# Logits of all heads in one TensorE step, PSUM handed out bank by bank, zero matmuls at the start

## The chip, the cores and the metric

The kernel runs on one core of one Trainium2 chip. The metric is device time in microseconds of one execution. A core has five engines that run side by side: TensorE (PE in the profile, with PEld for its weight loads), VectorE (DVE), ScalarE (ACT), GpSimd (POOL) and SyncE (SP, which here only issues DMAs). Matmuls write to PSUM, 128 partitions by eight banks; a bank holds 512 float32 per partition. VectorE and ScalarE copy results from PSUM to SBUF, the core's working memory.

## The reference

Two layers, each an attention block A and a gated mixing block B, both with a residual connection. The weights are the same in both layers.

```python
def _A_ref(x, wqkv, wo):              # x: 1 x 2048 x 576
    H = 32; Dh = 18; W, dil = (8, 2)
    qkv = (x @ wqkv).reshape(B, S, 3, H, Dh).transpose(2, 0, 3, 1, 4)
    q, k, v = qkv[0], qkv[1], qkv[2]
    idx = pos[:, None] - (arange(W) * dil)[None, :]     # 8 keys: t, t-2, ..., t-14
    mask = idx >= 0
    ...
    logits = einsum('bhsd,bhswd->bhsw', q, kg) * Dh ** -0.5
    attn = softmax(where(mask, logits, -1e9))
    o = einsum('bhsw,bhswd->bhsd', attn, vg)
    return o.transpose(0, 2, 1, 3).reshape(B, S, D) @ wo

def _B_ref(x, w_in, w_sp, b_sp, w_out):   # Fh = 2304
    z = gelu(x @ w_in)
    z1, z2 = z[..., :Fh], layernorm(z[..., Fh:])
    g = einsum('ts,bsf->btf', w_sp, z2) + b_sp[None, :, None]
    return (z1 * g) @ w_out

for _ in range(2):
    x = x + _A_ref(layernorm(x), A_wqkv, A_wo)
    x = x + _B_ref(layernorm(x), B_w_in, B_w_sp, B_b_sp, B_w_out)
```

All arrays are bfloat16; accumulation is float32.

## The kernel before

The program has five parts in a row: `phase_F(0)`, `phase_S(1)`, `phase_F(2)`, `phase_S(3)`, `phase_E()`.

**Phase F** holds, for one layer: the layer norm of x (16 row tiles of 128), the projections to q, k and v, the windowed attention, the output projection with the residual, a second layer norm, and z2 = gelu(x @ w_in) for the second half of w_in with its own layer norm. In layer two it begins with the last projection of block B of layer one (`p3_steps`). **Phase S** computes z1 and g = w_sp @ z2 for nine column blocks and multiplies them. **Phase E** is the last projection to the output.

Attention goes over 18 query tiles of 114 rows (each tile with a halo of 14 rows before it), in nine groups of two. Since the dilation is 2, even and odd rows (`par`) are independent and have 57 queries and 64 keys each. Head dimension 18 is laid on four row groups of 32 partitions, eight heads to a group. To bring q and k into that layout, `QK_steps` writes the projections to a DRAM buffer (`qk_bounce`) and reads them back as `QK`.

What sets the order is `Flow`, a planner that runs on the host while the program is built. Each piece of work is a `step` with an engine, a cost in microseconds, a key (its priority), the steps it comes after, and the buffers it takes and uses. `order()` places one step after another on the engine that is free first; `Plan` holds the keys' offsets, one set for each phase F. Phase S is written out by hand.

The steps that the change and the prediction touch:

- **Logits** (`Lm`, lines 615 to 628). For each query tile there are 64 matmuls of 18 x 64 keys against 18 x 57 queries, one for each of eight heads `g`, four row groups `j` and two parities; each goes to row group 32 j and to the upper or lower 64 columns of the array. They come in two steps, `La` for row groups 0 and 1 and `L` for 2 and 3, each with a PSUM buffer of two banks. Then follow exp on ScalarE (`x0`, `x1`), the mask on VectorE (`k`), P·V on TensorE (`v`, line 647) and the division by the sum (`f`).
- **PSUM** comes from a pool with two tags: `H`, three buffers of two banks, and `PT`, two buffers of one bank (`Ht`, `PTt`, `bank`, lines 256 to 263). The pool hands the buffers of a tag out in rotation. The planner counts how many are taken (`room`, `placed`), not which.
- **Waits**: the framework makes one instruction wait for another where they touch the same tile. `wrote_xn` and `read_xn_strided` (lines 242 to 254) drop waits between columns of `xnD` that do not overlap.
- **q and k, last 64 columns** (`mm4`, line 538): one bank's worth, in an `H` buffer.
- **g in phase S** (line 900): two halves of 16 matmuls each into the two banks of one `H` buffer; then for each half VectorE adds the bias (line 905) and multiplies by z1 (line 906).
- **p3** (line 362): 2 x 18 matmuls into an `H` buffer, 288 columns in each bank, then VectorE adds the residual (line 407). The last tile of phase E is added and stored in two halves.
- **Layer norm** (`ln_steps`): statistics on VectorE, small operations on GpSimd, normalisation on ScalarE, five transposes on TensorE (line 325), a copy by VectorE or ScalarE (lines 342 and 343, the lines of all such copies).

At the start VectorE's queue holds three small memsets, three memsets of the v buffers (line 801), and then the first statistics.

Of the kernel before, what the change touches and what calls it, by code (L numbers as in the profile page):

```python
# [18 lines left out]
P = 128  # L19
# [28 lines left out]
PLANS = (Plan(LX=4, LW=3.41, LR=3.7, KQ=4.95, KX=12.29,  # L48
              KV=2.02, KL=2.15, KE=22.44, KM=1.86, KP=2.02, KF=13.34, KY=2.53, KZ=15.66, KS=0.73, STAY=0.73, LF=4.38),
         Plan(LX=5.14, LW=3.5, LR=4.76, KQ=4.29, KX=10.53,  # L50
              KV=0.36, KL=2.04, KE=1.11, KM=0, KP=0.18, KF=6.22, KY=4.16, KZ=15.99, KS=0.47, STAY=0.73, LF=3.89))
# [3 lines left out]
class Flow:  # L55
# [31 lines left out]
    def room(self, st):  # L87

        t, more = 0.0, {}
        for tag, _ in st["takes"]:  # L90
            more[tag] = more.get(tag, 0) + 1
        for tag, n in more.items():
            ends = self.ends.setdefault(tag, [])
            left = self.caps[tag] - self.held.get(tag, 0) - n
            if left < 0:
                return None
            if left < len(ends):
                t = max(t, ends[-1 - left] + self.LAG)
        return t

    def placed(self, st):

        for tag, b in st["takes"]:
            self.held[tag] = self.held.get(tag, 0) + 1
            self.tag[b] = tag
        for b in st["uses"]:
            self.rest[b] -= 1
            self.last[b] = max(self.last.get(b, 0.0), st["end"])
            if not self.rest[b]:
                self.held[self.tag[b]] -= 1  # L110
                insort(self.ends.setdefault(self.tag[b], []), self.last[b])
# [8 lines left out]
    def order(self):  # L120
        free, mode = {}, {}
        self.ends, self.held, self.tag, self.last = {}, {}, {}, {}
# [64 lines left out]
    def issue(self):  # L187
        for st in self.order():
            st["fn"](st.get("arg", st["on"]))


class K:
# [17 lines left out]
    def setup(self):  # L210
# [4 lines left out]
        self.ps = ctx.enter_context(tc.tile_pool(name="ps", bufs=1, space=PSUM))  # L215
# [7 lines left out]
        make_identity(nc, self.ident[:])  # L223
        nc.vector.memset(self.neg_half[:], -0.5)
# [17 lines left out]
    def wrote_xn(self, ins, c0, c1):  # L242
# [4 lines left out]
        self.xn_writes.append((ins.ins, c0, c1))  # L247

    def read_xn_strided(self, ins, c0, c1):

        self.tc.declare_no_dep(ins.ins, group="xn_writes", keep=[w for w, a, b in self.xn_writes if a < c1 and c0 < b],
# [4 lines left out]
    def Ht(self, name):  # L256
        return self.ps.tile([P, 2, 512], f32, name=name, tag="H", bufs=3)

    def PTt(self, name):
        return self.bank(name)[:].bitcast(bf16)[:, 0:5 * P].rearrange("p (c n) -> p c n", n=P)  # L260

    def bank(self, name):
        return self.ps.tile([P, 512], f32, name=name, tag="PT", bufs=2)
# [29 lines left out]
    def ln_steps(self, fl, tag, key, row0, x, after, uses=(), guard=()):  # L293
# [27 lines left out]
        def trans(_):  # L321
            tp, xn = self.PTt("ln_tp"), box["xn"]
            box["tp"] = tp
# [5 lines left out]
        def evac(e):  # L329
            self.wrote_xn(self.copy(e, self.xnD[:, 0:5, cols], box["tp"][:, :, :n]), cols.start, cols.stop)  # L330
# [14 lines left out]
    def p3_steps(self, fl, i, key, wout, x_prev, x, takes, last):  # L345
# [8 lines left out]
        def mms(hh, part):  # L354
            def f(_):
                if hh == 0 and part == 0:
                    box["ps"] = self.Ht("p3_ps")
# [54 lines left out]
    def phase_F(self, li):  # L412
# [9 lines left out]
        fl = Flow(dict(H=3, PT=2, QK=3, bn=2, stg=6, xt=NX, xn=3, ln_st=6, o_t=2), pl.STAY, self.pairs, pl.LF)  # L422
# [84 lines left out]
        def QK_steps(g, key):  # L507
# [9 lines left out]
            for d in range(NM):  # L517
                def mm(rest_first, d=d):
                    ps = box[d] = self.Ht("qk_ps")
# [18 lines left out]
            def mm4(_):  # L538
                ps = box[NM] = self.Ht("qk4_ps")
                for c in range(NM + 1):  # L540
                    lhsT = wqk[:, c, NM * P:NM * P + P] if c < NM else wqk_r[:, NM * P:NM * P + P]
                    nc.tensor.matmul(ps[:, 0, 0:gw], lhsT=lhsT, rhs=self.xnD[:, c, at], start=(c == 0), stop=(c == NM))

            def ev4(e):
                box[NM, "s"] = stage()[:, 0:gw].rearrange("p (r j) -> p r j", r=2)
                self.copy(e, box[NM, "s"], box[NM][:, 0, 0:gw].rearrange("p (j r) -> p r j", r=2))
# [4 lines left out]
            fl.step(f"{tag}.m{NM}", "PE", 0.05 + 0.0021 * gw, key, mm4, feeds(c0, gw) + ["wqk", "wzero"],  # L551
                    takes=[("H", f"{tag}.ps{NM}")], mode="w", pairs=5)
# [22 lines left out]
        def V_steps(t, key):  # L575
            box, v = {}, vb[t % 3]

            def mm(rest_first):
                ps = box["ps"] = self.Ht("v_ps")
                c0 = QT * t  # L580

                def part(first, wide):
                    for c in range(NM) if wide else (NM,):
                        for s in range(2):
                            for par in range(2):
# [7 lines left out]
                                    tile_position=(rows.start, to.start)), c0, c0 + P)  # L593
# [15 lines left out]
        def ATT_steps(t, key):  # L609
# [5 lines left out]
            def Lm(a):  # L615
                def f(_):
                    qk = self.QKs[group[t]]
                    ps = box["L", a] = self.Ht("L_ps")
                    for g in (0, 2, 1, 3, 4, 6, 5, 7):
                        for par in range(2):  # L620
                            for j in (2 * a, 2 * a + 1):
                                rows = slice(32 * j, 32 * j + DH)
                                at, to = HP * (g // 2 % 2), 4 * par + 2 * (g // 4) + g % 2
                                nc.tensor.matmul(ps[at:at + HP, j % 2, to * QH:(to + 1) * QH],  # L624
                                                 lhsT=qk[rows, g, 1, par, kb:kb + HP],
                                                 rhs=qk[rows, g, 0, par, kb + HALO // 2:kb + HALO // 2 + QH],
                                                 start=True, stop=True, tile_position=(32 * j, at))
                return f
# [12 lines left out]
            def pv(_):  # L641
                O = box["O"] = self.Ht("O_ps")
# [8 lines left out]
            def fin(_):  # L651
# [10 lines left out]
            fl.step(tag + ".x0", "ACT", 0.92, key - pl.KE, ex(0), [tag + ".La", "fills"] + ([f"a{t - 2}.v"] if t > 1 else []), [tag + ".L0"],  # L662
                    mode="x")
            fl.step(tag + ".x1", "ACT", 0.92, key - pl.KE, ex(1), [tag + ".x0", tag + ".L"], [tag + ".L1"], mode="x")
# [6 lines left out]
            def tr(_):  # L671
                tp, o_t = self.PTt("o_tp"), box["o"]
# [19 lines left out]
        def W_steps(i):  # L692
# [5 lines left out]
            def wm(hh):  # L698
                def f(_):
                    if hh == 0:  # L700
                        box["ps"] = self.Ht("w_ps")
# [21 lines left out]
        def Z2_steps(i, key, after):  # L723
# [5 lines left out]
            def mm(u):  # L729
                def f(rest_first):  # L730
                    ps = box[u] = self.Ht("z_ps")
# [72 lines left out]
        fl.step("masks", "POOL", 2.0, -16, lambda _: fills(1), ["fills"] + (["lnx8.p"] if first else []))  # L804
        for i in range(NS):
# [16 lines left out]
        for i in range(NS):  # L822
            Z2_steps(i, pl.KZ + pl.KS * i, [f"win2.{k}" for k in range(len(win2_parts()))] +
                     ([] if first else [f"p3_{j}.m11" for j in range(NS)]))
        with tc.manual_schedule():
            fl.issue()
        self.pairs = fl.pairs
# [11 lines left out]
    def phase_S(self, li):  # L839
# [21 lines left out]
        for jj in range(NB):  # L861
# [7 lines left out]
            H3 = [self.Ht("z1_ps") for _ in range(3)]  # L869
            out = [[t[:, h, :] for h in range(2)] for t in H3]  # L870
            out.append([self.bank("z1_bank")[:] for _ in range(2)])
# [24 lines left out]
            for q in (range(4) if jj < NB - 1 else (3, 2, 1, 0)):  # L896
                ps = self.Ht("g_ps")
# [13 lines left out]
    def phase_E(self):  # L911
# [5 lines left out]
        fl = Flow(dict(H=3, x=4, ob=3))  # L917
# [9 lines left out]
        for i in range(NS):  # L927
            self.p3_steps(fl, i, i, wout, self.xres[1], lambda i=i: x_tile(i), [("x", f"x{i}")], True)
        with tc.manual_schedule():
            fl.issue()  # L930
        cm.__exit__(None, None, None)
# [57 lines left out]
```

## Time and profile before

| what | value |
|---|---|
| three runs | 1224.11, 1230.03, 1230.40 us, median 1230.03 |
| the profiled execution's own time | 1226.56 us |
| its span, first to last instruction | 1224.8 us |
| mean granted clock of TensorE | 0.997 |
| DMA traffic | 75.09 MB, mean 61 GB/s |

The profile shows one execution. In a row of the timeline stand: start and length in us, engine, line, operation, tile written and read, shape, count, and in brackets the idle time before it with what ended it. A matmul's row is longer than its share of TensorE: the matmuls overlap, so the cost of a group is read from its start to the next group's start. In a row of waits stand: who waited for whom, the total in us, how often, and the longest. "Granted clock" is the share of its full clock that TensorE was allowed. A wait for several things is put down to the one that came last.

### The profile page before, as it was taken

Reading aid. Unit: us, or ns where it says so; the run is one execution under the profiler, and the core shown is the slowest. Engines: PE = TensorE matmul, PEld = TensorE weight load, DVE = VectorE, ACT = ScalarE, POOL = GpSimd, SP = SyncE. Lnnn points to the kernel's source line nnn. Section 1 sums busy time; section 2 is a strip of 40 time slices with the busy share of each in tenths; the row PEclk is TensorE's granted clock in tenths of the full one; section 3 lists DMA queues with packets and bytes.
Section 4 is the critical chain, followed back from the end, with each engine's and each line's share of the span. In section 5 each row is a group of like instructions: output and inputs, shape, how many; then the busy total and the mean of one; then the engine's idle time right before and its main releaser. Section 6 shows DMA issues by size and latency. Waiting matters only on the chain.

```text
span 1224.8 us, 25328 instructions
## 1 busy us (share of the span) xinstructions
PE 1196.8 (98%) x10942; PEld 679.3 (55%) x10942; DVE 551.4 (45%) x894; ACT 396.8 (32%) x683; POOL 200.4 (16%) x492
## 2 busy tenths in 40 slices
PE   6899999999999999999999999999999999999998
PEld 4677655444444444448777776554444444444576
DVE  7787865423322232333466877652322332232311
ACT  6765687510011111003454767772111101111000
POOL 6211267400000000012111125671000000000000
PEclk9999999999999999999999999999999999999999
DMA  7655209430000000033323361088000000001121
GB/s 199 133 132 142 56 21 207 87 86 1 10 11 10 10 10 1 1 106 92 74 61 68 91 164 44 16 171 199 11 10 10 1 10 10 10 1 36 33 69 50
DMA packets 139649, 75.09 MB, mean 61 GB/s; under 512 B 96544, under 2 KB 136672, under 8 KB 139536
## 3 DMA queue, kind: packets, MB, share of 16 engines
q1 hardware_dynamic: 138864, 71.01, 24.5%
q0 software_dynamic: 672, 2.45, 0.8%
q8 instruction: 86, 1.41, 0.5%
q14 instruction: 27, 0.22, 0.1%
HBM read 39.54 MB, written 17.11 MB: 46 GB/s over the span
## 4 chain that ended last, share of the span: by engine, by line
PE 91%; DVE 3%; DMA 2%; ACT 1%; POOL 1%; SPq 1%; issue 1%; POOLq 0%; DVEq 0%
PE g_ps L900 41%; PE p_ps L362 11%; PE z_ps L288 11%; PE z_ps L876 8%; PE qk_ps L288 4%; PE w_ps L703 3%; PE v_ps L588 3%; PE z_bank L876 3%; PE z_ps L282 2%; PE O_ps L647 2%; DVE v_ext L342 1%; PE z_ps L882 1%; ACT v_ext L343 1%; PE ln_tp L325 1%; DMA QK<-qk_bounce 1%; PE qk_ps L282 1%
## 5 line engine op out<-in xcount | busy, mean ns | idle before, releaser
L900 PE MATMUL g_ps<-W,zu 128*128 128x512 bf16 x2304 | 500.2, 379 | 0.0
L900 PEld LDWEIGHTS <-zu 128*128 128x128 bf16 x2304 | 225.2, 98 | 272.1
L905 DVE TENSOR_TENSOR g_tmp<-g_ps,bsp 128x512 f32<-128x512 f32 x144 | 99.1, 688 | 432.4 <-PE g_ps L900 432.4
L892 ACT ACTIVATE zu<-z_ps 128x1024 bf16<-128x1024 f32 x54 | 51.4, 1025 | 516.0 <-PE z_ps L882 508.5
L362 PEld LDWEIGHTS <-zu 128*128 128x128 bf16 x1152 | 112.1, 98 | 32.1 <-DVE zu L906 2.1
L288 PE MATMUL z_ps<-wA,xnD 128*128 128x384 bf16 x576 | 109.8, 327 | 0.0
L362 PE MATMUL p_ps<-wA,zu 128*128 128x288 bf16 x768 | 105.8, 286 | 1.3 <-DVE v_ext L342 0.6
L906 DVE TENSOR_TENSOR zu<-g_tmp,zu 128x512 bf16<-128x512 f32 x144 | 99.7, 692 | 11.2 <-DVE g_tmp L905 0.5
L288 PEld LDWEIGHTS <-xnD 128*128 128x128 bf16 x768 | 70.9, 98 | 56.5 <-issue 14.6
L876 PE MATMUL z_ps<-xnD,w 128*128 128x512 bf16 x432 | 96.2, 378 | 0.0
L876 PEld LDWEIGHTS <-w 128*128 128x128 bf16 x576 | 54.2, 97 | 71.8 <-issue 8.0
L740 ACT ACTIVATE zu<-z_ps 128x768 bf16<-128x768 f32 x96 | 77.2, 805 | 33.0 <-PE z_ps L282 18.0
L750 DVE CUSTOM_DVE_ANT_1 zu<-zu 128x1536 bf16<-128x1536 bf16 x32 | 56.6, 1768 | 49.5 <-ACT zu L740 49.5
L288 PE MATMUL qk_ps<-xnD,wqk 128*128 128x242 bf16 x576 | 73.4, 274 | 3.5 <-ACT xnD L343 1.0
L632 ACT ACTIVATE P<-L_ps 128x912 bf16<-128x912 f32 x72 | 64.5, 940 | 7.1 <-PE L_ps L624 6.9
L308 POOL TENSOR_SCALAR ln_st<-ln_st 128x1 f32<-128x1 f32 x64 | 19.5, 304 | 273.9 <-DVE ln_st L304 226.3
L288 PEld LDWEIGHTS <-wqk 128*128 128x128 bf16 x576 | 54.2, 100 | 15.6 <-issue 9.9
L319 ACT ACTIVATE xn<-zu,ln_st 128x512 bf16<-128x512 bf16 (+1 forms) x56 | 33.3, 646 | 64.9 <-POOL ln_st L310 63.9
L801 POOL MEMSET v_ext<- 128x1216 bf16 x3 | 3.2, 1107 | 301.5 <-PE g_ps L900 301.5
L319 ACT ACTIVATE xn<-xt,ln_st 128x512 bf16<-128x512 bf16 x72 | 42.5, 646 | 23.8 <-POOL ln_st L310 23.8
L703 PE MATMUL w_ps<-wo,oT 128*128 128x288 bf16 x320 | 45.9, 293 | 2.0 <-DVE v_ext L342 1.5
L288 PE MATMUL z_ps<-wB,xnD 128*128 128x384 bf16 x192 | 46.9, 326 | 0.0
(88 smaller groups left out, 1141.1 us busy)
## 6 DMA issues: line engine op xcount, KB each, us to landing
qk_bounce<-stg SPq DMA_DIRECT2D x72, 121.0 KB
QK<-qk_bounce SPq DMA_DIRECT2D x72, 121.0 KB
w<-in_B_w_in_dram SPq DMA_DIRECT2D x36, 128.0 KB
wA<-in_B_w_in_dram SPq DMA_DIRECT2D x12, 288.0 KB
wA<-in_B_w_out_dram SPq DMA_DIRECT2D x4, 864.0 KB
xres<-xt SPq DMA_DIRECT2D x18, 144.0 KB
x<-xres SPq DMA_DIRECT2D x16, 144.0 KB
out_dram<-ob SPq DMA_DIRECT2D x15, 144.0 KB
```

The source lines that it names most:

```text
L288: nc.tensor.matmul(ps(s), lhsT=lhsT, rhs=rhs, start=(c == 0 and not rest_first), stop=(c == NM - 1 and rest_first))
L319: nc.scalar.activation(out=out, in_=in_, func=ACT.Identity, scale=rstd[:n], bias=nmr[:n])
L362: nc.tensor.matmul(ps[:, hh, 0:288], lhsT=u[:, s * S + i * P:s * S + (i + 1) * P], rhs=wout(b, s)[:, hh * 288:(hh + 1) * 288], start=(b == ...
L632: nc.scalar.activation(out=Psb[:, 2 * hh:2 * hh + 2, :, 0:QH], in_=box["L", hh][:, :, 0:8 * QH].rearrange("p a (b c) -> p a b c", c=QH), f ...
L703: nc.tensor.matmul(box["ps"][:, hh, 0:288], lhsT=oT[:, c, at:at + P], rhs=wo[:, c, hh * 288:(hh + 1) * 288], start=(c == 0), stop=(c == 4))
L740: nc.scalar.activation(out=self.zu[:, 3 * u:3 * u + 3, 256 * i:256 * (i + 1)].rearrange("p j (s r) -> p s j r", s=2), in_=box[u][:, :, 0:3 ...
L750: nc.vector.tensor_tensor_reduce(out=junk(0, 6), in0=z[:, 0:6, :], in1=z[:, 0:6, :], scale=1.0 / FH, scalar=0.0, op0=ALU.mult, op1=ALU.add ...
L876: nc.tensor.matmul(out[q][h], lhsT=w1[:, NM * h + c, :], rhs=self.xnD[:, c, PADL + 512 * q:PADL + 512 * q + 512], start=(first and c == 0) ...
L892: nc.scalar.activation(out=uq, in_=H3[q][:], func=ACT.Gelu_apprx_tanh)
L900: nc.tensor.matmul(ps[:, s, :], lhsT=z2[:, i, s, :], rhs=W[q][:, i, :], start=(i == 0), stop=(i == NS - 1))
L905: nc.vector.tensor_tensor(out=tmp[:], in0=ps[:, s, :], in1=bsp[:, 512 * q:512 * (q + 1)], op=ALU.add)
L906: nc.vector.tensor_tensor(out=uv, in0=tmp[:], in1=uv, op=ALU.mult)
```

## The change

1. `Lm(0)` and `Lm(1)` become one step `L` with both PSUM buffers. The loops are turned round so that eight matmuls in a row go to eight different places of the array: four row groups and two column halves.
2. PSUM is one tile of eight banks. The planner keeps the end time of each bank, picks the bank (`PT`) or the aligned pair (`H`) for each step in its computed order, and the step asks for what it was given. Any of the four pairs can be an `H` buffer and any bank a `PT` buffer. `mm4` takes one bank. Where waits on `xnD` are dropped, the writers whose PSUM bank a v projection takes over are kept. In phase S, which has no planner, the same rotation as before remains: pairs 0, 2, 4 and banks 6, 7.
3. Nineteen matmuls of zeros (12, 3 and 4) are put before the first layer norm's transposes, between the first and the second, and after the second. A memset of their operand comes first on VectorE.
4. The two plans' offsets are new.

```diff
+PLANS = (Plan(LX=4, LW=3.41, LR=3.7, KQ=5.26, KX=10.68,
+              KV=2.36, KL=2.02, KE=19.35, KM=1.6, KP=1.68, KF=13.78, KY=3.31, KZ=15.55, KS=0.38, STAY=0.5, LF=4.38),
...
+    def open_banks(self, tag):
+        w, f = 2 if tag == "H" else 1, self.bank_end
+        return [(max(f[k:k + w]), k) for k in range(0, 8, w) if None not in f[k:k + w]]
...
+            if tag in ("H", "PT"):
+                f = self.bank_end
+                fit = [(e, k) for e, k in self.open_banks(tag) if e + self.LAG <= st["start"] + 1e-9]
+                if tag == "H":
+                    k = min(fit)[1]
...
-        self.ps = ctx.enter_context(tc.tile_pool(name="ps", bufs=1, space=PSUM))
+        self.psum = ctx.enter_context(tc.tile_pool(name="ps", bufs=1, space=PSUM)).tile([P, 8, 512], f32, name="psum")
+        self.flow, self.turn = None, [0, 0]
...
+        self.idle = self.zu[:, NB, 0:512]
+        nc.vector.memset(self.idle, 0.0)
...
+    def banks(self, kind):
+        if self.flow is not None:
+            return self.flow.given(kind)
+        k = self.turn[kind == "PT"]
+        self.turn[kind == "PT"] += 1
+        return 6 + k % 2 if kind == "PT" else 2 * (k % 3)
+
+    def Ht(self):
+        b = self.banks("H")
+        self.last_bank = b
+        return self.psum[:, b:b + 2, :]
...
-                    for g in (0, 2, 1, 3, 4, 6, 5, 7):
-                        for par in range(2):
-                            for j in (2 * a, 2 * a + 1):
-                                rows = slice(32 * j, 32 * j + DH)
-                                at, to = HP * (g // 2 % 2), 4 * par + 2 * (g // 4) + g % 2
+                for g in (0, 1, 4, 5):
+                    for par in range(2):
+                        for s in range(2):
+                            for j in range(4):
+                                rows, gs = slice(32 * j, 32 * j + DH), g + 2 * s
+                                at, to = HP * s, 4 * par + 2 * (g // 4) + g % 2
...
-            fl.step(tag + ".La", "PE", 0.34, key - pl.KL, Lm(0), [f"qk{group[t]}a"] + ([f"a{t - 1}.L"] if t else []),
-                    [f"QK{group[t]}"], takes=[("H", tag + ".L0")], mode="q", pairs=H)
-            fl.step(tag + ".L", "PE", 0.34, key - pl.KL, Lm(1), [tag + ".La", f"qk{group[t]}"], [f"QK{group[t]}"], takes=[("H", tag + ".L1")],
-                    mode="q", pairs=H)
+            fl.step(tag + ".L", "PE", 0.36, key - pl.KL, Lm, [f"qk{group[t]}a", f"qk{group[t]}"], [f"QK{group[t]}"],
+                    takes=[("H", tag + ".L0"), ("H", tag + ".L1")], mode="q", pairs=2 * H)
...
+                    for k in range(n):
+                        nc.tensor.matmul(ps[:, k % 2, :], lhsT=self.idle[:, 0:P], rhs=self.idle, start=True, stop=True)
+                return f
+            for k, (n, cost, pre) in enumerate(((12, 5.2, []), (3, 0.7, ["lnx0.t", "spin0"]), (4, 0.9, ["lnx1.t", "spin1"]))):
+                fl.step(f"spin{k}", "PE", cost, -100, turn(n), pre, ["spin"] if k else [],
+                        takes=[] if k else [("H", "spin")], mode="w", pairs=n)
```

More of the change, by code (lines that the diff above doesn't have):

```diff
@@ L188, in issue, with given @@
         for st in self.order():
+            self.give = [(tag, self.bank_of[b]) for tag, b in st["takes"] if tag in ("H", "PT")]
             st["fn"](st.get("arg", st["on"]))
+    def given(self, kind):
+        tag, k = self.give.pop(0)
+        assert tag == kind
+        return k
 class K:
@@ L254, in read_xn_strided, with PTt, bank @@
         self.xn_strided.append((ins.ins, c0, c1))
[L256 to L263, printed above, removed]
+    def banks(self, kind):
[8 more added lines that the diff above has]
+        return self.psum[:, b:b + 2, :]
+    def PTt(self):
+        return self.bank().bitcast(bf16)[:, 0:5 * P].rearrange("p (c n) -> p c n", n=P)
+    def bank(self):
+        b = self.last_bank = self.banks("PT")
+        return self.psum[:, b, :]
     def load576(self, main, rest, lo, up, engs):
@@ L641, in pv @@
             def pv(_):
[L642 removed]
+                O = box["O"] = self.Ht()
                 for h in range(8):
@@ L671, in tr @@
             def tr(_):
-                tp, o_t = self.PTt("o_tp"), box["o"]
+                tp, o_t = self.PTt(), box["o"]
                 box["tp"] = tp
```

106 lines of the change are left out of this document (66 added, 40 removed).

## The prediction

> **What bounds the kernel now.** I read the page's first part and its chain of waits, then one table of stretches, then single stages.
>
> ```profile
> span 1224.8 us, 25328 instructions
> PE 1196.8 (98%) x10942; PEld 679.3 (55%) x10942; DVE 551.4 (45%) x894; ACT 396.8 (32%) x683; POOL 200.4 (16%) x492
> PE 91%; DVE 3%; DMA 2%; ACT 1%; POOL 1%; SPq 1%; issue 1%; POOLq 0%; DVEq 0%
> ```
>
> TensorE is busy 98% of the span and makes 91% of the chain. Time can come from three places only: less TensorE work, TensorE work at a better clock, or the 28 us in which it stands. The stretches below follow the phases: start, two pieces of fill, attention, the z2 matmuls, the mixing phase S, then the same for layer two, and the last projection. Columns: length, then busy time (and instructions) of PE, PEld, DVE, ACT, POOL, granted clock, DMA share, GB/s.
>
> ```profile
> core 0: us, PE busy (x) PEld busy (x) DVE busy (x) ACT busy (x) POOL busy (x), PEclk, DMA share, GB/s
> 0.00:8.00 8.00, 0.00 (x0) 0.00 (x1) 5.13 (x12) 2.15 (x3) 2.68 (x12) 1.00 0.79 211
> 8.00:28.00 20.00, 18.34 (x178) 13.38 (x178) 15.81 (x43) 15.18 (x28) 14.63 (x46) 1.00 0.79 203
> 28.00:46.00 18.00, 15.12 (x363) 11.13 (x361) 13.71 (x26) 13.10 (x22) 8.22 (x20) 0.91 0.63 123
> 46.00:148.00 102.00, 96.98 (x2288) 75.30 (x2287) 82.61 (x144) 64.70 (x102) 13.96 (x36) 0.98 0.52 119
> 148.00:228.00 80.00, 80.00 (x562) 42.42 (x561) 47.78 (x64) 63.92 (x142) 55.26 (x133) 1.00 0.42 89
> 228.00:548.50 320.50, 320.50 (x1513) 142.53 (x1512) 96.66 (x144) 36.35 (x49) 9.48 (x22) 1.00 0.12 29
> 548.50:603.00 54.50, 53.74 (x476) 42.84 (x475) 24.62 (x50) 17.70 (x28) 9.48 (x27) 1.00 0.35 97
> 603.00:748.00 145.00, 140.03 (x2925) 110.42 (x2923) 105.14 (x184) 85.52 (x130) 25.86 (x57) 1.00 0.40 92
> ...
> 1149.00:1224.78 75.78, 71.07 (x577) 56.17 (x575) 14.96 (x21) 0.00 (x0) 0.00 (x0) 0.99 0.18 56
> ```
>
> The z2 stretch and phase S have no idle TensorE, so nothing the change does to waits can help there. The idle time sits in the first 46 us (8.0 + 1.7 + 2.9), in the two attention stretches (5.0 each), at the start of layer two (0.8) and in the last stretch (4.7).
>
> **Part 1, the logits.** Before, a step issues 32 matmuls for two head columns; after, one step issues 64 over all four row groups and both column halves.
>
> ```profile
> 46.41 0.69 PE L647 MATMUL O_ps<-v_ext,P 128*64 128x38 bf16 x32
> 46.94 1.15 PE L588 MATMUL v_ps<-wv,xnD 128*64 128x288 bf16 x16
> ...
> 48.27 0.73 PE L624 MATMUL L_ps<-QK 18*64 18x57 bf16 x64
> 48.94 0.45 PE L675 MATMUL o_tp<-ident,o_t 128*128 128x128 bf16 x5
> ...
> 99.82 0.45 PE L624 MATMUL L_ps<-QK 18*64 18x57 bf16 x31
> 100.20 0.45 PE L675 MATMUL o_tp<-ident,o_t 128*128 128x128 bf16 x5
> ```
>
> From start to the next start, 64 logits matmuls cost 48.94 - 48.27 = 0.67 us and 32 cost 0.38, so 32 more cost 0.29: 9.1 ns each, with 0.09 fixed. The P·V matmuls above cost 0.53 for 32, or 16.6 ns. Those alternate over two tiles, so each tile is used once in 33 ns; the logits go round four tiles (two row groups, both halves within eight matmuls), once in 36 ns each, although 57 columns stream instead of 38. The pace thus looks like a tile's own turnaround, not the number of columns. Eight tiles would give 36/8 = 4.5 ns, and 64 x 4.5 + 0.09 = 0.38 us. The other bound: if 9.1 ns is what two instructions cost to issue, the step stays at 0.67. I take 0.40, near the tile reading since P·V, with the same two instructions per matmul, goes by tiles. Over 36 steps: 36 x (0.67 - 0.40) = **-9.7 us**, bounds -10.4 and 0.
>
> The Trainium skill speaks on both sides here. "TensorEngine Tiling (Array Packing)", Instruction Overhead, gives each matmul about 60 cycles whatever its columns; read per instruction that is 25 ns at its 2.4 GHz, 1.6 us for 64, and more tiles gain nothing, but the trace's 0.67 us contradicts it, and only a reading per tile fits. "TensorE: Matmul & The Clock Gate", Part 3, puts starts on different tiles about 4 ns apart: an estimate of 0.35 us with the fixed 0.09, or -11.5 us.
>
> **Part 2, PSUM as eight banks of one tile.** Waits now follow the banks that two instructions share. Before, they followed a whole two-bank buffer: both halves, whoever was needed, and the buffers in fixed rotation.
>
> ```profile
> 548.68 0.69 DVE L905 TENSOR_TENSOR g_tmp<-g_ps,bsp 128x512 f32<-128x512 f32 x1 [4.16 <-PE g_ps L900]
> ...
> 550.73 0.69 DVE L906 TENSOR_TENSOR zu<-g_tmp,zu 128x512 bf16<-128x512 f32 x1
> 551.48 0.30 PE L362 MATMUL p_ps<-wB,zu 128*128 128x288 bf16 x1 [0.76 <-DVE zu L906]
> ...
> 1152.02 0.30 PE L362 MATMUL p_ps<-wBe,zu 128*128 128x288 bf16 x1 [0.76 <-DVE zu L906]
> ...
> 1220.23 0.41 PE L362 MATMUL p_ps<-wA,zu 128*128 128x288 bf16 x2 [0.55 <-DVE ob L407]
> ```
>
> VectorE's add of the first half starts only at 548.68, when all 32 g matmuls have run. By the waits in the two programs it waits for the sixteenth after the change. Then only the second half is left at 548.68: add and multiply, 2 x 0.69 and a little between, end near 550.1, before the matmul that stood from 550.72 to 551.48. The wait goes at both ends of phase S: -1.5 us. At 1220.23 the second half of the last tile stood behind the add of the first half; the program after has no such wait: -0.55. Together **-2.1 us**, bounds -2.1 and -0.5 (only the last is left if the adds still run late).
>
> ```profile
> PE w_ps L703 <- DVE v_ext L342: 1.5, 4, 0.5
> PE O_ps L647 <- DVE v_ext L342: 1.4, 4, 0.4
> PE qk_ps L288 <- DVE v_ext L342: 1.0, 3, 0.5
> ```
>
> In attention these 3.9 us are matmuls that want a buffer which the v copies still held. After, the computed order hands out the bank that it knows to be free. But a logits step now takes four banks at once, and the retuned plan is another order with waits of its own. I take **-3 us**; bounds -10 (all idle time of both attention stretches) and +3 (as much again).
>
> **Part 3, zero matmuls at the start.** They add 19 matmuls of 128x512, a small memset ahead of VectorE's queue, and a wait for the first layer norms' transposes.
>
> ```profile
> 3.77 1.07 DVE L801 MEMSET v_ext<- 128x1216 bf16 x1 [0.20 <-issue]
> 4.75 0.76 DVE L303 BATCH_NORM_STATS2 ln_st<-zu 128x6 f32<-128x288 bf16 x2
> ...
> 10.83 1.77 PE L288 MATMUL qk_ps<-xnD,wqk 128*128 128x242 bf16 x8 [0.78 <-ACT xnD L343]
> ...
> 13.05 2.93 PE L288 MATMUL qk_ps<-xnD,wqk 128*128 128x242 bf16 x16
> ...
> 29.51 1.00 PE L288 MATMUL qk_ps<-xnD,wqk 128*128 128x242 bf16 x8
> ...
> L900 PE MATMUL g_ps<-W,zu 128*128 128x512 bf16 x2304 | 500.2, 379 | 0.0
> ```
>
> The same eight matmuls take 1.77 us at 10.83 and 1.00 at 29.51: TensorE runs slow at first, though the granted clock reads 1.00 there. At full speed the eight would be 0.8 us shorter and the sixteen at 13.05 (twice 1.00, less the overlap: about 1.9) 1.0 us: 1.8 together. Against that stands the memset: 512 elements at the rate of v_ext's (1.07 for 1216) are 0.45 us, on VectorE just ahead of the first statistics, which start as soon as the memsets end. Net -1.3 on TensorE. The layer norms behind (DVE 15.8 and ACT 15.2 of 20 us from 8 to 28) don't speed up, so I take **-0.9**; bounds -1.8 and +1.3. The upper end is zero matmuls that do not speed TensorE up: one takes 500.2/2304 = 0.22 us at full speed, 0.43 at half, so the last four, which stand between the second transposes and the first projection, run 0.9 us longer than the gap allows, and the memset adds 0.45.
>
> The Trainium skill's "TensorE: Matmul & The Clock Gate", Part 1, says that the clock is at half until about 3.4 us of sustained matmuls have run; by it, twelve cold zero matmuls (an estimate of 5.1 us) are enough, and the sum would take -1.3. The trace agrees as far as the slow first matmuls go.
>
> **Given back.** In the attention stretch VectorE is busy 82.6 and ScalarE 64.7 of 102 us. With some 7 us less TensorE time there, VectorE would be at 87%, so copies come later. I let the idle time of each attention stretch grow by 1.5: **+3 us**, bounds 0 and +8.
>
> **The clock** fell to half twice:
>
> ```profile
> 28.99:32.41 3.42, 2.51 (x127) 2.00 (x131) 3.26 (x9) 2.90 (x6) 2.71 (x9) 1.00 0.38 104
> 32.41:35.82 3.41, 3.41 (x50) 2.20 (x38) 2.33 (x5) 3.41 (x6) 2.87 (x7) 0.50 0.35 73
> ...
> 141.64:145.05 3.41, 3.41 (x17) 2.11 (x15) 3.14 (x4) 2.17 (x4) 1.43 (x3) 0.50 0.02 5
> ```
>
> Each dip of 3.41 us loses half of it, 1.7 us, after a stretch in which TensorE stood for about a quarter. The new order may have none, or four: 0, bounds -3.4 and +3.4.
>
> **Sum:** -9.7 - 2.1 - 3 - 0.9 + 3 = -12.7 us against the profiled execution's own 1226.56 us (span 1224.8, the rest around it), so **1214 us**. The median of the three runs, 1230.03, lies 3.5 above that execution and the lowest 2.4 below; a spread of 6.3 us, as much as four dips, so I leave the sum at 1214.
>
> **The rivals.**
> *Copies bind in attention.* For it: VectorE's 81% and waits that name v copies. Against: ScalarE has room and takes part of these copies. Half of the logits' 9.7 comes back: 1219 us.
> *The logits step is no faster* (the change does not do what it says): issue sets 9.1 ns. For it: nothing shows two such matmuls closer on average. Against: the tile arithmetic. 1214 + 9.7 = 1224 us.
> *The instruction supply binds, and the kernel gets slower.*
>
> ```profile
> q8 instruction: 86, 1.41, 0.5%
> ```
>
> 86 packets feed 10942 matmuls, 127 each; attention uses one per 5.7 us (2288 matmuls in 102 us). A faster logits step takes 64 of these in 0.4 us, with 32 of P·V and 20 of v close by. If a packet then comes late, TensorE stands in each of the 36 steps. It turns the kernel slower from (12.7 + 6)/36 = 0.52 us per step; at 0.65 the time is 1237. Against it: the number of matmuls is the same and the mean need rises by only 7%.
>
> **How the numbers follow.** Forecast 0.60, copies 0.14, logits no faster 0.12, supply 0.09, others 0.05. About 0.5% (6 us) is what can be told from no change, so faster means under 1224: forecast, copies and half of the third case, 0.80; same 0.10; slower 0.10. The forecast's own range is 1206 to 1221. The range for 8 in 10 reaches from 1200 (logits 0.38, all waits for buffers gone, no dips, nothing given back) to 1230 (logits no faster, and +3 in place of -3 for the buffers).
>
> **What would show it.** Right: logits groups of 64 near 0.40 us to the next start; no 0.76 us wait after phase S and no 0.55 us wait at the end; the first eight projections near 1.0 us; TensorE's busy time down by some 8 to 10 us. Wrong: logits at 0.67; attention stretches with over 7 us idle each; waits by "issue" on TensorE behind the logits; more than two stretches at clock 0.50.

## The result and the profile after

| kernel | runs | median us | lowest to highest | profiled execution | its span |
|---|---|---|---|---|---|
| before | 5 | 1225.20 | 1224.11 to 1230.40 | 1226.56 | 1224.8 |
| after | 5 | 1215.67 | 1214.38 to 1217.65 | 1215.67 | 1214.0 |

The ratio of the two is 0.9911, with a 95% interval from 0.9883 to 0.9939: faster by 0.9%, 1.7 us above the forecast. The forecast change was -12.7 us; the profiled executions differ by 10.9, the medians by 9.5. So the total came near, but most of its terms did not. First the page of after, its first part and its chain of waits:

```profile
span 1214.0 us, 25394 instructions
PE 1192.3 (98%) x10899; PEld 679.2 (56%) x10961; DVE 560.7 (46%) x900; ACT 398.7 (33%) x680; POOL 203.4 (17%) x492
PE 93%; DVE 2%; DMA 2%; ACT 1%; issue 1%; SPq 1%; DVEq 0%; ACTq 0%
```

TensorE still sets the end, with a larger share of the chain, 93% for 91%. Its busy time is down by 4.5 us only, and it now contains the zero matmuls. The stretches of after, cut at about the same points of the work (columns as before):

```profile
0.00:8.00 8.00, 4.20 (x12) 1.43 (x12) 5.33 (x13) 1.90 (x2) 2.44 (x12) 0.98 0.76 206
8.00:28.00 20.00, 19.40 (x197) 14.18 (x198) 17.01 (x47) 15.82 (x30) 14.44 (x45) 0.92 0.78 205
28.00:46.00 18.00, 15.06 (x331) 10.95 (x330) 10.28 (x20) 12.55 (x21) 8.19 (x22) 0.81 0.53 123
46.00:143.00 97.00, 94.84 (x2341) 74.29 (x2315) 82.88 (x145) 70.32 (x106) 15.21 (x39) 1.00 0.57 125
143.00:222.00 79.00, 79.00 (x558) 42.11 (x558) 48.56 (x64) 62.05 (x139) 58.88 (x129) 1.00 0.21 44
222.00:542.20 320.20, 318.35 (x1481) 142.65 (x1510) 101.17 (x146) 36.23 (x49) 9.55 (x23) 1.00 0.17 41
542.20:596.80 54.60, 54.60 (x484) 43.71 (x482) 23.63 (x49) 17.02 (x27) 9.53 (x27) 1.00 0.36 95
596.80:742.00 145.20, 141.36 (x2808) 109.05 (x2807) 107.14 (x190) 85.65 (x131) 26.83 (x65) 1.00 0.40 93
...
1139.60:1213.97 74.37, 70.78 (x578) 56.26 (x575) 13.67 (x19) 0.00 (x0) 0.00 (x0) 0.99 0.19 57
```

The holes in phase S (320.20 less 318.35) are matmul records missing from the trace: 1481 matmuls stand beside 1510 weight loads. With the same holes in layer two's phase S (1.7 us) they make 3.6 of the 4.5 us by which the busy time fell, so TensorE's work, zero matmuls included, is shorter by about 1 us. From its first matmul to the first one behind it, phase S of layer one takes 320.58 us in both kernels. Where the 10.8 us of span went, from the same stretches and the starts of the phases:

- Layer one up to phase S: 227.9 before, 221.7 after, -6.2.
- Layer two up to phase S: 279.9 before, 276.8 after, -3.1.
- From the last g matmul to the end: 75.8 before, 74.3 after, -1.5.

By kind: TensorE's idle time in layer one's attention (28 to 148 us before, 28 to 143 after) fell from 2.88 + 5.02 to 2.94 + 2.16, by 2.8; the ends of phase S and of the kernel gave 2.1, the start 1.25, the logits some 2.6 (all below). That is 8.7. The other 2.1 weren't traced to single steps.

**The logits.** The timeline of after, TensorE alone:

```profile
45.80 0.70 PE L675 MATMUL psum<-QK 18*64 18x57 bf16 x64
46.43 1.00 PE L338 MATMUL psum<-xnD,wqk 128*128 128x242 bf16 x8
...
105.69 0.70 PE L675 MATMUL psum<-QK 18*64 18x57 bf16 x64
106.32 0.45 PE L723 MATMUL psum<-ident,o_t 128*128 128x128 bf16 x5
```

A group of 64 costs 46.43 - 45.80 = 0.63 us over eight places, where the prediction's row has 0.67 over four and its forecast 0.40. One row is the shortest kind: over all groups that ran without a stop the mean per 64 is 0.65 us, and 0.73 before, where 42 groups stand in place of 36 (some were cut in two, at 0.09 each). That is 36 x 0.07, some 2.6 us.

**The end of phase S.** The timeline of after, both engines:

```profile
542.26 1.63 PE L412 MATMUL psum<-wA,zu 128*128 128x288 bf16 x12
542.46 0.69 DVE L967 TENSOR_TENSOR g_tmp<-psum,bsp 128x512 f32<-128x512 f32 x1 [2.04 <-PE psum L962]
543.19 0.69 DVE L968 TENSOR_TENSOR zu<-g_tmp,zu 128x512 bf16<-128x512 f32 x1
543.73 0.90 PE L412 MATMUL psum<-wB,zu 128*128 128x288 bf16 x6
```

Now only one add and one multiply follow the last g matmul; they are done at 543.88, while the twelve wA matmuls still run, and no wait stands in the TensorE rows. The first half was added earlier, as foretold.

**The start.** TensorE in the first microseconds of after:

```profile
1.25 4.20 PE L860 MATMUL psum<-zu 128*128 128x512 bf16 x12 [1.25 <-DVE zu L261]
8.25 0.72 PE L375 MATMUL psum<-ident,xn 128*128 128x128 bf16 x5 [2.80 <-ACT xn L369]
8.76 1.49 PE L860 MATMUL psum<-zu 128*128 128x512 bf16 x3
10.04 0.74 PE L375 MATMUL psum<-ident,xn 128*128 128x128 bf16 x5
10.58 1.25 PE L860 MATMUL psum<-zu 128*128 128x512 bf16 x4
11.66 0.99 PE L338 MATMUL psum<-xnD,wqk 128*128 128x242 bf16 x8
```

The first eight projections take 0.99 us, not 1.77, but start at 11.66, not 10.83. The third transposes, which follow the projections of the first two row tiles, start at 14.87 in this trace and at 16.12 in before's: 1.25 us earlier. This point moves from execution to execution: in five profiles with these zero matmuls (after, e1, e3, e4, e7 below) it lies between 14.18 and 15.43, in six without (before, e2, e5, e6, e9, e10) between 15.37 and 16.71.

**The waits** of TensorE in after (who waits for whom: total, times, longest):

```profile
PE psum L375 <- ACT xn L369: 2.8, 1, 2.8
PE psum L675 <- DMA QK<-qk_bounce: 2.5, 3, 1.6
...
PE psum L697 <- DVE v_ext L392: 0.7, 3, 0.2
PE psum L697 <- ACT v_ext L393: 0.7, 2, 0.4
PE psum L675 <- issue: 0.7, 1, 0.7
...
PE psum L697 <- issue: 0.5, 1, 0.5
```

All waits of TensorE for v copies came to 5.9 us before (the 3.9 us that the prediction shows are the three largest rows); all rows for the copies of lines 392 and 393 come to 2.6 us after. The largest one left in attention is for the q and k data themselves.

### The profile page after: what moved, and what is told of

It reads as the page before. It is cut to its first block, busy times and chain, and to the rows that moved or that the text cites. A ratio compares the mean times of both kernels' runs of the same rounds, so it can differ in the third digit from the quotient of the medians.

```text
span 1214.0 us, 25394 instructions
## 1 busy us (share of the span) xinstructions
PE 1192.3 (98%) x10899; PEld 679.2 (56%) x10961; DVE 560.7 (46%) x900; ACT 398.7 (33%) x680; POOL 203.4 (17%) x492
## 4 chain that ended last, share of the span: by engine, by line
PE 93%; DVE 2%; DMA 2%; ACT 1%; issue 1%; SPq 1%; DVEq 0%; ACTq 0%
PE psum L962 41%; PE psum L338 15%; PE psum L412 12%; PE psum L938 10%; PE psum L638 3%; PE psum L751 3%; PE psum L332 3%; PE psum L697 2%; PE psum L944 1%; PE psum L675 1%; PE psum L375 1%; DVE v_ext L392 1%; ACT v_ext L393 1%; SPq L243 1%; PE psum L592 1%
## 5 line engine op out<-in xcount | busy, mean ns | idle before, releaser
L962 PE MATMUL psum<-W,zu 128*128 128x512 bf16 x2256 | 497.7, 379 | 2.5
L967 DVE TENSOR_TENSOR g_tmp<-psum,bsp 128x512 f32<-128x512 f32 x144 | 99.6, 692 | 428.0 <-PE psum L962 423.9
L954 ACT ACTIVATE zu<-psum 128x1024 bf16<-128x1024 f32 x54 | 51.4, 1024 | 517.0 <-PE psum L944 508.5
L938 PE MATMUL psum<-xnD,w 128*128 128x512 bf16 x562 | 129.0, 378 | 2.2 <-ACT zu L788 1.0
L338 PE MATMUL psum<-wA,xnD 128*128 128x384 bf16 x576 | 109.8, 327 | 0.8 <-DVE xt L457 0.3
L412 PE MATMUL psum<-wA,zu 128*128 128x288 bf16 x768 | 105.9, 286 | 0.1
L788 ACT ACTIVATE zu<-psum 128x768 bf16<-128x768 f32 x96 | 77.3, 806 | 30.8 <-PE psum L332 16.5
L338 PE MATMUL psum<-xnD,wqk 128*128 128x242 bf16 x576 | 71.3, 271 | 1.0 <-DVE ln_st L354 0.3
L682 ACT ACTIVATE P<-psum 128x912 bf16<-128x912 f32 x72 | 64.0, 944 | 18.3 <-PE psum L675 15.7
L338 PE MATMUL psum<-wB,xnD 128*128 128x384 bf16 x192 | 46.9, 326 | 0.0
```

What stands on the lines that cost most here:

```text
L338: nc.tensor.matmul(ps(s), lhsT=lhsT, rhs=rhs, start=(c == 0 and not rest_first), stop=(c == NM - 1 and rest_first))
L412: nc.tensor.matmul(ps[:, hh, 0:288], lhsT=u[:, s * S + i * P:s * S + (i + 1) * P], rhs=wout(b, s)[:, hh * 288:(hh + 1) * 288], start=(b == ...
L682: nc.scalar.activation(out=Psb[:, 2 * hh:2 * hh + 2, :, 0:QH], in_=box["L", hh][:, :, 0:8 * QH].rearrange("p a (b c) -> p a b c", c=QH), f ...
L788: nc.scalar.activation(out=self.zu[:, 3 * u:3 * u + 3, 256 * i:256 * (i + 1)].rearrange("p j (s r) -> p s j r", s=2), in_=box[u][:, :, 0:3 ...
L938: nc.tensor.matmul(out[q][h], lhsT=w1[:, NM * h + c, :], rhs=self.xnD[:, c, PADL + 512 * q:PADL + 512 * q + 512], start=(first and c == 0) ...
L954: nc.scalar.activation(out=uq, in_=H3[q][:], func=ACT.Gelu_apprx_tanh)
```

## The experiments

Two theories were open after this. *Issue*: a weight load and its matmul take a fixed time to issue, so the eight places gain nothing and the gain is made by the banks, the offsets and the start. *Order*: a single part, above all the offsets, makes all of it. Each ratio below is to the kernel before on the same chip, with its 95% interval.

| label | kernel | median us | ratio |
|---|---|---|---|
| e1 | after, once more | 1214.03 | 0.9905 (0.9881 to 0.9930) |
| e2 | after without zero matmuls | 1216.68 | 0.9913 (0.9894 to 0.9932) |
| e3 | after, logits over four places at a time | 1215.09 | 0.9906 (0.9885 to 0.9927) |
| e4 | after, three fixed pairs and two fixed banks | 1223.43 | 0.9969 (0.9957 to 0.9981) |
| e5 | before, one tile of eight banks, same banks | 1224.76 | 0.9979 (0.9967 to 0.9991) |
| e6 | before with the new offsets | 1240.21 | 1.0104 (1.0084 to 1.0124) |
| e7 | after, half the query columns left out | 1213.65 | one run |
| e8 | after, 25 and 12 zero matmuls | 1217.63 | 0.9922 (0.9906 to 0.9938) |
| e9 | before with banks picked by the computed order | 1221.58 | 0.9957 (0.9945 to 0.9970) |
| e10 | e9 with one logits step | 1222.70 | 0.9963 (0.9950 to 0.9976) |
| e11 | after, start kept warm by 128 more zero matmuls | 1216.46 | 0.9918 (0.9905 to 0.9931) |
| e12 | after, 64 small zero matmuls more | 1214.37 | 0.9899 (0.9886 to 0.9912) |

### What sets the pace of the logits: e3 and e7

e3 keeps one step but walks the places as before; e7 streams 28 columns in place of 57 and leaves the other queries out. The nested loops are written in one line here.

```diff
e3:
-for g in (0, 1, 4, 5):  for par in range(2):  for s in range(2):  for j in range(4):
+for a in range(2):  for g in (0, 1, 4, 5):  for s in range(2):  for par in range(2):  for j in (2 * a, 2 * a + 1):
e7:
-rhs=qk[rows, gs, 0, par, kb + HALO // 2:kb + HALO // 2 + QH],
+rhs=qk[rows, gs, 0, par, kb + HALO // 2:kb + HALO // 2 + 28],
...
```

> The changed kernel with the logits still in one step of 64, but walked as before: row groups 0 and 1 first, then 2 and 3, so four array places in any eight matmuls. If instruction issue sets the pace: 0.67 us per group instead of 0.63, in all 36 x 0.04 = 1.4 us slower. If the eight places matter more than the group's row shows: 0.75 us or more per group and 4 us or more slower.

> The changed kernel with logits matmuls of 28 query columns instead of 57; the other queries' logits and exponentials are left out, and the P tiles are filled with ones once. If issue sets the pace: a group of 64 still takes 0.60 to 0.63 us. If streaming or the turnaround of an array place does: 0.45 us or less.

The timeline of e3:

```profile
103.59 0.73 PE L676 MATMUL psum<-QK 18*64 18x57 bf16 x64
104.25 0.45 PE L724 MATMUL psum<-ident,o_t 128*128 128x128 bf16 x5
```

and of e7:

```profile
104.72 0.68 PE L675 MATMUL psum<-QK 18*64 18x28 bf16 x64
105.33 0.46 PE L723 MATMUL psum<-ident,o_t 128*128 128x128 bf16 x5
```

Four places 0.66, eight 0.63, eight with half the columns 0.61; the means over all groups without a stop are 0.71, 0.65 and 0.63. Half the columns save some 0.02 us, the eight places 0.06. In 36 groups the places are worth 2 us, which e3's ratio, the same as e1's within their intervals, can't show.

Read one by one, a group has two halves. The first 0.14 us of one group in after and in e3, the logits alone (length, busy time and matmuls of PE, the same of PEld, clock, DMA share, GB/s):

```profile
105.69:105.83 0.14, 0.14 (x32) 0.14 (x33) 1.00 0.15 42
103.59:103.73 0.14, 0.14 (x16) 0.14 (x20) 1.00 0.36 90
```

In the same time 32 matmuls start over eight places and 16 over four. From start to start that is 4.5 and 8.4 ns for the first 32 pairs of weight load and matmul, so a place takes a new pair once in 34 to 36 ns; it is 4.5 with half the columns too (e7), and 16.1 on the two places of P·V, once in 32. Then comes a gap (some 95 ns from start to start over eight places, 70 over four), and the last 32 pairs go 8.3 ns apart over eight places and 8.5 over four, again with 28 columns as with 57. The break is not one of the order of heads: when a group over eight places is stopped inside, the next 32 pairs are close again. e11 (below) has a stop after 22 matmuls, and then:

```profile
709.71:709.85 0.14, 0.14 (x31) 0.14 (x33) 1.00 0.21 62
```

So some 32 pairs look as if they were waiting when a group begins, and these go at the pace of the places. Behind them one pair comes in 8.3 ns, and more places gain nothing. The issue theory holds for the second half of a group and not for the first. Whether the sequencer or the weight load sets the 8.3 ns, no run tells apart. The 4 ns between tiles, which the prediction quoted from the Trainium skill, "TensorE: Matmul & The Clock Gate", Part 3, is seen in the first half (3 to 4 ns within a round of eight places) and not behind it: the prediction's estimate was 0.35 us per group against 0.63 measured.

### Banks alone: e5

All of before's order and buffers, but as banks of one tile, so that waits follow banks.

```diff
...
-        return self.ps.tile([P, 2, 512], f32, name=name, tag="H", bufs=3)
+        b = self.last_bank = int(next(self.pairs_of))
+        return self.psum[:, b:b + 2, :]
...
```

> The kernel before with one thing changed: PSUM is one tile, every step writes the very banks it wrote before, so that only the waits become those of the banks touched. If waits by bank are worth what the phase ends show: 0.76 + 0.76 + 0.55 = 2.1 us faster than before and nothing in attention. If they also empty the attention stretches: 4 to 6 us faster, with the PE waits on v copies (3.9 us) mostly gone.

The stretch of e5 after phase S of layer one, then TensorE's waits for v copies:

```profile
548.50:603.00 54.50, 54.50 (x507) 43.46 (x509) 23.30 (x48) 17.70 (x28) 9.48 (x27) 1.00 0.35 98
```

```profile
PE psum L707 <- DVE v_ext L346: 1.6, 4, 0.5
...
PE psum L651 <- DVE v_ext L346: 1.3, 4, 0.4
PE psum L292 <- DVE v_ext L346: 1.1, 3, 0.5
```

No idle time is left after phase S (0.76 before). The median is 1.9 us below before's on the same chip; the ratio says 2.6, from 1 to 4. The waits for v copies are those of before (1.5, 1.4, 1.0): with the same buffers, waiting by bank doesn't help them.

### Free banks and offsets: e4, e6, e9, e10

e4 takes the free choice away from after (the planner computes its order anew); e6 gives only the new offsets to before; e9 gives before the free banks but neither the offsets, the one step nor the zero matmuls; e10 is e9 with the one step.

```diff
e4:
-        return [(max(f[k:k + w]), k) for k in range(0, 8, w) if None not in f[k:k + w]]
+        return [(max(f[k:k + w]), k) for k in (range(0, 6, 2) if tag == "H" else range(6, 8)) if None not in f[k:k + w]]
e6, to before:
-PLANS = (Plan(LX=4, LW=3.41, LR=3.7, KQ=4.95, KX=12.29,
+PLANS = (Plan(LX=4, LW=3.41, LR=3.7, KQ=5.26, KX=10.68,
...
```

> The changed kernel with PSUM divided as before (three pairs for H, two banks for PT), still handed out by the computed order. If the freedom to use any bank is what emptied the attention stretches of waits: 3 to 5 us slower, with waits on v copies back at 2 us or more. If the bank-level waits or the new offsets did it: within 1 us.

> The kernel before with the changed kernel's two plans' offsets and nothing else. If the offsets alone made the better order: 2 to 4 us faster than before. If they only fit the changed steps: within 1 us, or slower.

> The kernel before (two logits steps, its offsets, no zero matmuls) with PSUM handed out by the computed order from all eight banks, and with waits by bank. Waits by bank alone gave 2.0 us. If the freedom to take any bank empties the attention stretches whatever the offsets: 4 to 6 us faster than before. If it needs offsets tuned for it: 2 us or less, or slower.

> The same as the run before it in this list, and the logits of all heads in one step; still the offsets of before and no zero matmuls. If the one step is worth what its rows show (0.04 us per group of 64 and fewer cut groups): 1.5 to 2 us faster than that run. If the two are within 1 us, the rest of the way to the changed kernel without zero matmuls (1216.7 us) is the offsets'.

TensorE's waits in e4:

```profile
PE psum L697 <- DVE v_ext L392: 2.4, 8, 0.3
```

and two attention stretches of e6:

```profile
603.00:748.00 145.00, 137.53 (x2825) 108.14 (x2812) 104.73 (x187) 84.05 (x123) 24.01 (x60) 1.00 0.39 92
748.00:839.00 91.00, 84.96 (x649) 45.42 (x648) 51.16 (x68) 64.65 (x140) 57.34 (x129) 0.98 0.14 32
```

Fixed buffers cost after some 8 us (0.9969 for 0.9905), and eight P·V groups wait for v copies on VectorE (2.4 us; 0.7 in after). That is 1.7 of the 8; the rest wasn't traced, and as e4 keeps offsets that were found with the free choice, it doesn't price the free choice alone. The new offsets alone cost before 13 us: TensorE stands 7.5 and 6.0 us in these stretches of layer two, which before lost 5.0 and none. Free banks with the old offsets give 5.3 us in all, some 2.7 beyond e5 (0.9957 for 0.9979; the intervals overlap at their ends, so the size is loose). One logits step adds nothing to that (0.9963). So the offsets are worth some 6 us on top of free banks (e2's 1216.68 beside e10's 1222.70, each against its own before: 10.7 less 4.2; the ratios' intervals are apart) and are a loss without them. The theory that one part makes all of it falls. In e10's profile layer two is the shortest of all kernels (274.7 us to its phase S, after 276.8) and layer one long (227.1): the new offsets for layer one with the old ones for layer two weren't tried. That profile is of e10's shortest execution, 3.4 us under its median, so the 274.7 flatters it.

### The zero matmuls and the clock: e1, e2, e8, e11

e2 leaves out the zero matmuls and their memset. e8 has 25 in place of 12 at the start and 12 more before the first logits. e11 does the same with 128 more, 114 of them small, and keeps after's order.

```diff
e8:
+for k in range(12 if first and t == 0 else 0):
+    nc.tensor.matmul(box["L", 0][:, k % 2, :], lhsT=self.idle[:, 0:P], rhs=self.idle, start=True, stop=True)
...
```

> The changed kernel once more, as the yardstick for the runs beside it. Both theories expect 9 to 11 us under the kernel before, logits groups of 64 at 0.63 us to the next start, and no wait of 0.76 us after phase S.

> The changed kernel without the nineteen zero matmuls and their memset. If warming TensorE pays: 1.5 to 2.5 us slower than the changed kernel, the first eight projection matmuls at 1.77 us instead of 0.99, the first projection group done at about 16.1 us instead of 14.9. If the zero matmuls only trade slow projections for a later start (11.66 against 10.83 us), and the fill behind is set by DMAs: within 0.7 us of the changed kernel, with PE idle for QK later instead.

> The changed kernel with 25 zero matmuls in the first piece instead of 12, and 12 more ahead of the first logits, into the same banks. If half clock after idle stretches costs what the rows show: no stretch at clock 0.50 from 7.6 to 11 us and from 31.5 to 38.3 us, the first projection at 10.7 to 11.0 us instead of 11.66, and 2 to 4 us faster than the changed kernel. If the fill is set by DMAs all the same: no dips, but within 1 us.

> The changed kernel with TensorE kept busy in its two idle stretches at the start: 14 zero matmuls of 512 columns and 114 small ones in the first piece, and 12 ahead of the first logits. Together they are 128 more than in the changed kernel, so that every later instruction stands at the same place of its block of 128, and the order is the same. If half clock is what is lost there: no stretch at clock 0.50 before 45 us, layer two as in the changed kernel (276.7 us), and 2 to 3 us faster than it. If DMAs set the fill: within 1 us.

Up to phase S, layer one takes 221.7 and 219.9 us in the two profiles of after and 222.5 in e2's; the medians differ by 1.0 and 2.65, where e1's six runs alone reach from 1212.85 to 1220.49. The ratios (0.9911 and 0.9905 for after, 0.9913 without) don't tell the two apart: the traces show an earlier start, but a gain in time by the zero matmuls is not shown. The clock in after (columns as in the other stretches):

```profile
4.20:7.60 3.40, 1.25 (x6) 0.39 (x4) 2.66 (x7) 0.48 (x2) 1.23 (x4) 1.00 1.06 323
7.60:11.00 3.40, 2.75 (x14) 1.62 (x15) 1.20 (x3) 2.36 (x5) 0.90 (x3) 0.50 0.96 243
28.00:31.50 3.50, 1.24 (x10) 0.60 (x8) 2.27 (x7) 2.44 (x5) 2.77 (x9) 1.00 0.65 137
31.50:34.90 3.40, 3.21 (x75) 2.05 (x76) 0.37 (x1) 2.43 (x4) 2.76 (x8) 0.50 0.20 48
```

The clock record begins at 4.2 us with 1.00, 3.0 us after the first zero matmul (in e1 at 5.8, 4.6 after it), so twelve are enough. But TensorE then stands for 2.8 us, and from 7.6 it runs at half. e11 fills that gap, and its first projections start at 10.98:

```profile
10.98 0.99 PE L338 MATMUL psum<-xnD,wqk 128*128 128x242 bf16 x8
```

It has no half clock before 711 us and layer one takes 219.5 us. Yet it is no faster than after: layer two takes 281.0 us in its profile, 4.3 more than e1's. Its timeline there:

```profile
706.66 0.29 PE L677 MATMUL psum<-QK 18*64 18x57 bf16 x22
709.71 0.52 PE L677 MATMUL psum<-QK 18*64 18x57 bf16 x42 [2.76 <-issue]
```

A group of 64 breaks after 22 matmuls and goes on 2.76 us later, with no semaphore between; half clock follows from 711.3 to 714.7 and costs an estimated 1.7, half of its 3.41. Together 4.5, about the 4.3 that were lost. What came late shows in the DMA queues of e11 (packets, MB, share), first from 696.6 to 706.6, then from 706.6 to 710:

```profile
q1 hardware_dynamic: 1571, 1.84, 76.5%
...
q1 hardware_dynamic: 354, 0.30, 68.0%
q8 instruction: 1, 0.02, 3.0%
```

Queue q8 brings TensorE's instructions: it has 86 packets in after and 87 in e11, which has 128 matmuls more. In ten microseconds it brought nothing (in e1's same stretch, two packets). The next packet starts at 706.62, ends at 708.25, and TensorE resumes 1.46 us after. Why it was late isn't settled. The DMA engines of e11 were full just before (a share of 1.09 from 704 to 707, where e1 has 0.70):

```profile
704.00:707.00 3.00, 2.96 (x56) 2.13 (x51) 2.58 (x4) 2.31 (x5) 0.00 (x0) 1.00 1.09 155
```

e8's layer two is 281.6 us long too. Its order differs from after's; layer two has a 0.5 us wait by issue and 3.4 us at half clock (its 1.1 us wait by issue is in layer one). The rest wasn't traced.

### Is the instruction supply at its limit: e12

An instruction packet carries 128 pairs or so; 64 small zero matmuls more shift all that follows by half of that, in the same order.

```diff
+for k in range(0 if n < 70 else 64):
+    nc.tensor.matmul(ps[HP * (k % 2):HP * (k % 2) + HP, 0, 0:38], lhsT=self.idle[:, 0:HP], rhs=self.idle[:, 0:38], ...)
```

> The changed kernel, same order, with 64 small zero matmuls more in the first piece, in time in which TensorE stands anyway. They only move every later instruction by half a block of 128. If the instruction supply limits the attention stretches, and the order was fitted to where the blocks end: 3 to 8 us slower, most of it in layer two, with idle time behind logits and P.V groups. If the supply has room: within 1 us.

1214.37 us, the same as after: with the packets' ends half a packet elsewhere the kernel takes the same time, so they don't hold it as a rule. But e10, with nothing shifted, shows the break of e11 twice, in its timeline around 50 and 105 us:

```profile
51.66 0.24 PE L696 MATMUL psum<-v_ext,P 128*64 128x38 bf16 x4 [1.34 <-issue]
...
105.89 0.26 PE L674 MATMUL psum<-QK 18*64 18x57 bf16 x15 [1.05 <-issue]
```

In both, an instruction packet ends 1.4 and 1.65 us earlier, as in e11. This holds for all 21 waits by issue of 0.4 us or more in the fourteen traces of the runs told here: each ends 1.25 to 1.96 us after the end of a packet on q8, while these packets come once in some 6 us in attention. So the supply is late now and then: 1.2 us in after's profile (the rows of 0.7 and 0.5 by issue above), 2.4 in e10's, 3.3 in e11's, 0.5 in before's.

## Why the prediction was right, and where not

**Logits, -9.7: wrong.** The step that failed is "Eight tiles would give 36/8 = 4.5 ns, and 64 x 4.5 + 0.09 = 0.38 us". A place's turnaround was read rightly, and 4.5 ns is what eight places reach, but for the first 32 pairs only. The rest go at 8.3 ns whatever the places, behind a gap of 0.1 us. The prediction took places and issue as two readings of which one must be true ("if 9.1 ns is what two instructions cost to issue, the step stays at 0.67"); each holds for half of a group. Over four places both give nearly the same pace, 8.4 and 8.5 ns, so the rows of before could not part them; single starts would have shown the two halves. The term is some -2.6. The rival "the logits step is no faster" came closer to what happened; its price of 1224 us was wrong because it left the other terms as they were.

**Ends of phase S and of the kernel, -2.1: right.** -2.1 in the traces, -1.9 in e5's median, and by the mechanism named: the first half's add no longer waits for the last g matmul.

**Buffers in attention, -3, and given back, +3: the net of 0 was wrong.** Free banks bring some -2.7 over e5, near the forecast -3, but the offsets that go with them bring some -6 more (e2 and e10), and nothing was given back: attention's idle time fell by 2.8 us in layer one and hardly moved in layer two (4.97 to 3.84, with a new wait of 1.0 at the end of the z2 stretch). The "given back" term rested on the 7 us that the logits never gave. The prediction treated the plan's offsets as a cost to be bounded, not as a term; only e4 and e6 show that they fit the free banks and not fixed buffers.

**Start, -0.9: right in size in the traces, not shown in the time.** -1.25 from before's trace to after's; over all traces the third transposes come at 14.2 to 15.4 with zero matmuls and at 15.4 to 16.7 without. The pieces differ: the memset took 0.27 us, not 0.45, and the zero matmuls between the transposes ran at half clock behind the 2.8 us gap; with the gap filled (e11) they did not.

**Clock, 0: right on the whole.** Half clock for 3.4 and 6.8 us in after's profile, 3.4 twice in e1's, beside 3.4 twice and an unrecorded slow start in before's.

**Rivals.** Copies don't bind: TensorE's idle time fell although VectorE is busy 82.9 of 97 us, 85%, in attention. The instruction supply does stop TensorE, but a few times in an execution, not at each of the 36 steps, and not by the eight places: e3 and after have it alike (waits by issue at the logits of 0.8 and 0.7 us).

So the total came near by luck: a term 7 us too large was nearly made up by one of some 6 us that was missing and 3 us of losses that didn't come. The runs' own terms don't add up either. Logits -2.6, ends -2.1, free banks -2.7, offsets -6 and start -1.25 make -14.7, where the traces have -10.8. They overlap (the one step by itself gains nothing in e10), and some are loose by a few us; which of them shrink together stays open.

## What to carry to other kernels

For streams of tiny matmuls, read the single starts before crediting a gain to tiling: here the places set the pace of the first 32 pairs of weight load and matmul, and behind them a pair took 8.3 ns over any number of places. Then change one size (columns, places) at a time. PSUM as one tile with hand-picked banks pays twice, by waits that follow banks and by a free choice of banks, but the order's tuning must be made with that freedom, and tested with it: the same offsets were worth some 6 us with it and cost 13 without. When TensorE breaks off inside a group with no semaphore, look at its instruction queue, not at its operands.

## What the runs showed of the hardware

- Half clock doesn't need a wholly idle stretch: it followed 3.4 us in which TensorE was busy for 37% (1.25 of 3.40, after) and, in before, for 73% (2.51 of 3.42). In after it stayed for a second 3.4 us in which TensorE was busy for 94% (3.21 of 3.40).
- The first 32 pairs of weight load and matmul of a group, or behind a stop, go at the pace of the places: 16.1 ns a pair over two places (P·V), 8.4 over four, 4.5 over eight, so once in 32 to 36 ns in each place, with 57 columns as with 28. Behind these a pair comes no closer than 8.3 ns on average, whatever the places and columns.
- A late instruction packet stopped TensorE for up to 2.76 us. All 21 waits by issue of 0.4 us or more end 1.25 to 1.96 us after the packet's end.
